# A one-token attention and FFN kernel: wq in two transfers, the Exp table loaded in the preamble, block 0's softmax chain ahead of K1's transposes, and the two halves of H back to back

## The chip, the core and the metric

The kernel runs on one core of a Trainium2 chip. The metric is the time of one execution on the device in microseconds; the median of three runs is 112.3 us.

The engines are named as in the profile: PE is TensorE, DVE is VectorE, ACT is ScalarE, POOL is GpSimd, and SP is SyncE, which here only issues transfers.

## What is computed

Two rows x (batch 2, one token, D = 448) go through a normalisation, attention over a window of a cache, a small FFN, and a gate:

```python
W = min(4096, max(256, Sk // 4))                       # 2048 of 8192 cached positions
q = (xn @ wq).reshape(B, Sq, 16, 256)                  # xn = layernorm(x); wq [448, 4096]
scores = einsum("bhqd,bhkd->bhqk", q, k) * 256 ** -0.5 # 8 K/V heads, each used by 2 query heads
o = einsum("bhqk,bhkd->bhqd", softmax(scores), v)
s = o.reshape(B, Sq, 4096) @ wo                        # wo [4096, 448]
g = silu(relu(xn @ w1) @ w2)                           # w1 [448, 1792], w2 [1792, 448]
out = x + s * g
```

Everything is bf16 in memory. K and V of the window are 33.6 MB of the 44.1 MB that the kernel reads; wq and wo are 3.7 MB each, w1 and w2 1.6 MB each.

## The kernel before

**Blocks.** The 16 pairs of batch and K/V head are worked on in four blocks of four pairs (`NQ = 4`). K and V of a block are one transfer each of 4 MB, 32 KB for each of the 128 partitions: 32 groups of 64 positions by 4 pairs. There are two K buffers (`kbuf`), one V buffer (`vbuf`), one buffer for weights (`wbuf`: first wq, later w1 and w2), and wo goes into `kbuf[0]` at the end.

**What one block does.** `do_T` (L424) transposes K in eight pieces on DVE (`kt`). `do_S` (L432) makes the scores on PE: one matmul that sets a mask (`wcol`, `wrow`), then 32 of 128x512 into the bank `sbk`, four for each transposed piece. The softmax chain follows: `ch_max` (row maximum, DVE), `ch_rmT` (transpose of the maxima, PE), `ch_mrow` (maximum per pair and a copy, DVE), `ch_exp` (a small matmul, a bias copy and the Exp on ACT, then a sum over partitions on PE), `ch_pt` (transpose of the weights `pt` and the reciprocal of the sum, DVE). `do_PV` (L446) multiplies with V (32 matmuls into `obk`), scales by the reciprocal on ACT (`o_sb`), and folds; `do_at` stores the block's result. `do_qbd` (L360) places the query of a block on POOL.

**The order.** Each engine runs a list of its own, written out by hand: an engine works strictly in the order in which the operations are recorded at L499 to L601, and waits on semaphores. On PE the sections S, PV and CH are loops over the same code, in the order PRO, S(0), CH(0), S(1), PV(0), CH(1), S(2), PV(1), CH(2), S(3), PV(2), CH(3), FFN, PV(3), WO, END. On DVE, block 0's chain is interleaved with the transposes of K1 (L508 to L520): T(1,0), maximum, T(1,1), mrow, T(1,2), T(1,3), T(1,4), pt, reciprocal, T(1,5) to T(1,7). For the later blocks the chain stands ahead of the next block's transposes.

**Transfers.** SP issues all large ones on one queue, in this order: wq, K0, K1, V0, K2 (after K0's last transpose), V1 (after PV(0)), K3 (after K1's last transpose), V2, w1, w2 (after PV(1)), V3 (after PV(2)), and wo in four parts. ACT issues the two small loads of x and the store.

**Start.** ACT clears four banks, DVE makes the statistics of x, ACT takes the square root (L312), DVE builds the normalised row in the layout of the projection (`xr`, L347). `do_q` (L357) multiplies it with wq in seven slots of four matmuls (28 into `fbk`), DVE scales and transposes the query.

**FFN.** `do_H(0)` and `do_H(1)` (L380) are seven matmuls each, for two halves of the hidden row, into `fbk` and `cbk`; after each DVE writes the relu into `h_n`. `do_hT` (L391) transposes `h_n` at once and copies it into `h_sb` in four pieces; `do_F` multiplies with w2 (14 matmuls), `do_gate` applies silu. **End.** The folded result is multiplied with wo: 26 wide matmuls into `wbk` (the first 18 need wo's first part, eight more its second), a copy `wsum` (L575), 4 matmuls that add it and 24 narrow ones into `cbk`, of which the last ones need wo's last parts; then DVE multiplies with the gate (L595), adds x and ACT stores.

All matmuls but one are recorded by the helper `mm`, so the profile has them on L354.

Of the kernel before, what the change touches and what calls it, by code (L numbers as in the profile page):

```python
# [6 lines left out]
F32 = mybir.dt.float32  # L7
ACT = mybir.ActivationFunctionType
# [149 lines left out]
def bass_recurrent_scan__sliding_block_cached__dense_activation_relu__decode_kernel(  # L158
# [34 lines left out]
    with es:  # L193
# [26 lines left out]
        xt = named("xt", [128, SLOTS * 128], BF)  # L220
        st6 = named("st6", [128, 6], F32)
        st2 = named("st2", [128, 2], F32)
        sd = named("sd", [128, 2], F32)
        rstd = named("rstd", [128, 1], F32)
        xr = named("xr", [128, SLOTS * 4], BF)
        qn = named("qn", [128, 512], BF)
# [52 lines left out]
        def load_v(k):  # L279
# [3 lines left out]
        p_xc = pr.op(POOL, lambda e: e.memset(x_c[:, :], 0.0))  # L283
        d_xc = pr.dma(ACTE, view(x_c, 0, [[1, NCOL]], n=8, pstep=16),
                      A_x[:, 0, :].rearrange("b (i n) -> i b n", i=4), [p_xc], key="v")
        d_wq = pr.dma(SP, wbuf[:, :], wq_src)
        load_k(0)
        load_k(1)
        load_v(0)
# [10 lines left out]
        for t0 in (h_sb, h_n, ea, ga):  # L300
# [9 lines left out]
        v_ve = pr.op(DVE, lambda e: e.tensor_scalar(  # L310
            out=sd[0:B, 0:1], in0=st2[0:B, 1:2], scalar1=EPS, scalar2=None, op0=ALU.add), [v_ag])
        a_sd = pr.op(ACTE, lambda e: e.activation(sd[0:B, 1:2], sd[0:B, 0:1], ACT.Sqrt), [v_ve])  # L312
        v_rs = pr.op(DVE, lambda e: e.reciprocal(rstd[0:B, :], sd[0:B, 1:2]), [a_sd])
        for e2 in range(2):
            v_xn = pr.op(DVE, lambda e, e2=e2: e.tensor_scalar(
# [39 lines left out]
                                      skip_group_check=True, **kw)  # L355

        def do_q():  # L357
            deps = [d_wq, v_xr]
            for s in range(SLOTS):
                for i in range(4):  # L360
                    lo = s * HC + i * 512
                    o = pr.op(PE, mm(fbk[32 * i:32 * i + 4, :], xr[:, 4 * s:4 * s + 4], wbuf[:, lo:lo + 512],
                                     s == 0, s == SLOTS - 1, tile_position=(0, 32 * i)), deps)
                    deps = []
            st["q_mm"] = o
            v = pr.op(DVE, lambda e: e.tensor_scalar(
                out=view(qn, 0, [[64, 8], [32, 2], [1, 32]]),
                in0=view(fbk, 0, [[64, 8], [1, 2], [2, 32]]),
                scalar1=SCALE, scalar2=None, op0=ALU.mult), [o])
            st["qT"] = pr.op(DVE, lambda e: e.transpose(qt[:, :], qn[:, :]), [v])  # L370
# [7 lines left out]
                deps = []  # L378

        def do_H(u):  # L380
            deps = [d_w1] if u == 0 else [st["h_n"]]
            for s in range(SLOTS):
                lo = s * FC + u * (FC // 2)
                o = pr.op(PE, mm((fbk, cbk)[u][0:4, 0:FC // 2], xr[:, 4 * s:4 * s + 4], wbuf[:, lo:lo + FC // 2],
                                 s == 0, s == SLOTS - 1), deps)
                deps = []
            st["h_n"] = pr.op(DVE, lambda e: e.tensor_scalar(  # L387
                out=view(h_n, 32 * u, [[64, 14], [1, 32]], n=4), in0=view((fbk, cbk)[u], 0, [[1, 14], [14, 32]], n=4),
                scalar1=0.0, scalar2=None, op0=ALU.max), [o, p_z])

        def do_hT():  # L391
            v = pr.op(DVE, lambda e: e.transpose(ht[0:32, :], h_n[0:32, :]), [st["h_n"]])  # L392
            for hf in range(2):
                for u in range(2):
                    st["hT"] = pr.op(DVE, lambda e, hf=hf, u=u: e.tensor_copy(  # L395
                        view(h_sb, 0, [[1, 14], [16, 2]], n=32, p0=64 * hf + 32 * u),
                        view(ht, 32 * u + hf, [[64, 14], [2, 2]], n=32)), [v, p_z])

        def do_F():
            deps = [d_w2, st["hT"]]  # L400
# [104 lines left out]
        do_S(0)  # L505
        load_k(2)
        do_qbd(1)
        do_T(1, 0)  # L508
        ch_max(0)
        do_T(1, 1)  # L510
        pr.section("CH", 0)
        ch_rmT(0)
        ch_mrow(0)
        do_T(1, 2)
        ch_exp(0)
        do_T(1, 3)
# [115 lines left out]
```

## Time and profile before

| | |
|---|---|
| runs | 112.3, 113.17, 112.0 us; median 112.3 |
| the profiled execution | 112.89 us, of which the span from the first to the last instruction is 111.6 |
| mean granted TensorE clock | 0.816 |
| busy | PE 66.5 us (60%), DVE 58.3 (52%), ACT 14.7 (13%), POOL 7.2 (6%) |
| read from memory | 44.11 MB, 395 GB/s over the span; the SP queue's packets fill 93.2% of 16 engines' time |

How to read the rows: a row of the timeline has the start, the length, engine and line, the operation as result<-operands, the shapes and a count; the bracket at its end is the idle time of the engine before it and what ended that. A row of the windows has the stretch, its length, the busy time (and count) of PE, PEld (weight loads), DVE, ACT and POOL, the granted clock, the DMA share and GB/s; a packet is counted where it begins. The slices of the page are 40 equal parts of the span, the busy share and the granted clock in tenths. A row of DMA issues has the queue, the size, and the median time from issue to landing.

### The profile page before, as it was taken

Reading aid. Unit: us, or ns where it says so; the run is one execution under the profiler, and the core shown is the slowest. Engines: PE = TensorE matmul, PEld = TensorE weight load, DVE = VectorE, ACT = ScalarE, POOL = GpSimd, SP = SyncE. Lnnn points to the kernel's source line nnn. Section 1 sums busy time; section 2 is a strip of 40 time slices with the busy share of each in tenths; the row PEclk is TensorE's granted clock in tenths of the full one; section 3 lists DMA queues with packets and bytes.
Section 4 is the critical chain, followed back from the end, with each engine's and each line's share of the span. In section 5 each row is a group of like instructions: output and inputs, shape, how many; then the busy total and the mean of one; then the engine's idle time right before and its main releaser. Section 6 shows DMA issues by size and latency. Waiting matters only on the chain.

```text
span 111.6 us, 1080 instructions
## 1 busy us (share of the span) xinstructions
PE 66.5 (60%) x412; PEld 25.7 (23%) x412; DVE 58.3 (52%) x94; ACT 14.7 (13%) x32; POOL 7.2 (6%) x31
## 2 busy tenths in 40 slices
PE   0000570069952399992499992349994579099461
PEld 0000110024411233431233431113431312034120
DVE  1089331199979992022799722299952220900531
ACT  2940000000001600004100003200002300002600
POOL 6500003000030000030000030000000000000000
PEclk9999999557999557999656999656999755558999
DMA  6899999999999999976899899899889989979940
GB/s 164 350 443 430 446 423 446 446 411 423 470 411 399 470 435 411 446 305 188 388 493 435 376 458 482 376 423 505 388 378 432 530 376 399 517 330 436 384 189 1
DMA packets 2188, 44.11 MB, mean 395 GB/s; under 512 B 266, under 2 KB 396, under 8 KB 652
## 3 DMA queue, kind: packets, MB, share of 16 engines
q1 hardware_dynamic: 2160, 44.11, 93.2%
q10 hardware_dynamic: 28, 0.01, 0.0%
HBM read 44.11 MB, written 0.00 MB: 395 GB/s over the span
## 4 chain that ended last, share of the span: by engine, by line
DMA 46%; PE 35%; DVE 9%; ACT 4%; issue 3%; SPq 1%; DVEq 0%; ACTq 0%
DMA kbuf<-in_A_k_cache_dram 46%; PE sbk L354 17%; PE fbk L354 6%; PE obk L354 5%; PE cbk L354 3%; DVE kt L429 3%; PE nbk L354 2%; SPq L46 1%; PE wbk L354 1%; ACT o_sb L455 1%; ACT L485 1%; DVE h_n L387 1%; DVE ht L392 1%; ACT e_sb L485 1%; PE mbk L354 1%
## 5 line engine op out<-in xcount | busy, mean ns | idle before, releaser
L354 PE MATMUL sbk<-kt,qbd 128*128 128x512 bf16 x128 | 36.2, 447 | 11.0 <-DVE kt L429 10.9
L429 DVE STREAM_TRANSPOSE kt<-kbuf 128x1024 f32<-128x1024 f32 x32 | 36.8, 1206 | 7.0 <-DMA kbuf<-in_A_k_cache_dram 7.0
L354 PEld LDWEIGHTS sbk<-kt,qbd 128*128 128x128 bf16 x128 | 13.5, 110 | 33.7 <-issue 22.0
L354 PE MATMUL fbk<-wbuf,xr 128*4 128x512 bf16 (+1 forms) x35 | 5.9, 614 | 12.4 <-DVE xr L347 12.4
L354 PE MATMUL obk<-vbuf,pt 128*16 128x512 bf16 x128 | 8.2, 379 | 0.0
L455 ACT ACTIVATE o_sb<-obk,rs 128x512 bf16<-128x512 f32 x4 | 2.7, 687 | 40.2 <-PE obk L354 40.2
L375 POOL COPY qbd<-qt 32x64 bf16<-32x64 bf16 x16 | 3.8, 240 | 58.2 <-PE sbk L354 44.8
L467 DVE TENSOR_REDUCE rm<-sbk 128x1 f32<-128x512 f32 x4 | 2.7, 682 | 8.7 <-PE sbk L354 8.7
L354 PE MATMUL fbk<-wbuf,h_sb 128*17 128x448 bf16 x14 | 4.6, 505 | 2.9 <-DVE h_sb L395 2.9
L354 PE MATMUL nbk<-ssum,gsum 128*128 128x1 f32 x8 | 2.1, 337 | 5.8 <-ACT e_sb L485 5.8
L490 DVE STREAM_TRANSPOSE pt<-e_sb 128x512 bf16<-128x512 bf16 x4 | 2.8, 698 | 4.8 <-ACT e_sb L485 4.8
L484 ACT ACTIVATE bias<-mbk 128x1 f32<-128x1 f32 x4 | 0.7, 171 | 33.4 <-PE mbk L354 33.4
L354 PEld LDWEIGHTS fbk<-wbuf,xr 128*4 128x4 bf16 x35 | 1.6, 114 | 15.0 <-DMA wbuf<-in_A_wq_dram 12.4
L494 DVE TENSOR_TENSOR at_exp<-nbk,qmask 128x64 bf16<-128x64 f32 x4 | 0.9, 225 | 7.2 <-PE nbk L354 7.2
L354 PEld LDWEIGHTS obk<-vbuf,pt 128*16 128x16 bf16 x128 | 3.1, 88 | 4.3 <-issue 1.3
L354 PE MATMUL mbk<-one_f,mrow 1*128 1x1 f32 x8 | 1.5, 256 | 3.4 <-DVE mrow L479 3.4
L415 DVE TENSOR_SCALAR ea<-ea 128x112 f32<-128x112 f32 x1 | 0.2, 219 | 5.8 <-ACT ea L409 5.8
L354 PE MATMUL nbk<-fold,o_sb 128*128 128x8 bf16 x16 | 1.0, 173 | 3.7 <-ACT o_sb L455 3.7
L354 PEld LDWEIGHTS nbk<-ssum,gsum 128*128 128x128 f32 x8 | 1.8, 280 | 6.1 <-ACT e_sb L485 6.1
L354 PE MATMUL cbk<-wbuf,xr 128*4 128x448 bf16 x7 | 2.8, 574 | 0.7 <-DVE h_n L387 0.7
L354 PEld LDWEIGHTS fbk<-wbuf,h_sb 128*17 128x17 bf16 x14 | 1.6, 121 | 6.2 <-issue 6.0
L409 ACT ACTIVATE ea<-fbk 17x112 f32<-17x112 f32 x4 | 1.0, 252 | 14.4 <-PE fbk L354 14.3
(74 smaller groups left out, 42.1 us busy)
## 6 DMA issues: line engine op xcount, KB each, us to landing
kbuf<-in_A_k_cache_dram SPq DMA_DIRECT2D x4, 4096.0 KB, 21.2
vbuf<-in_A_v_cache_dram SPq DMA_DIRECT2D x4, 4096.0 KB
wbuf<-in_A_wq_dram SPq DMA_DIRECT2D x1, 3584.0 KB, 11.5
wbuf<-in_B_w_dram SPq DMA_DIRECT2D x2, 1568.0 KB, 20.0
kbuf<-in_A_wo_dram SPq DMA_DIRECT2D x1, 2016.0 KB, 19.0
kbuf<-in_A_wo_dram SPq DMA_DIRECT2D x1, 896.0 KB, 20.6
kbuf<-in_A_wo_dram SPq DMA_DIRECT2D x1, 448.0 KB, 21.2
kbuf<-in_A_wo_dram SPq DMA_DIRECT2D x1, 224.0 KB, 21.3
```

The lines of the kernel that those rows point to most:

```text
L46: o = _Op(eng, lambda e: e.dma_start(dst, src), deps, True, key)
L354: return lambda e: e.matmul(out_ap, lhsT=lhsT, rhs=rhs, start=start, stop=stop, skip_group_check=True, **kw)
L375: st["qbd", k] = pr.op(POOL, lambda e, a=a: e.tensor_copy(view(qbd, 24 + 32 * a, [[128, 8], [2, 4], [1, 2]], n=32, p0=32 * a), view(qt, 0, ...
L387: st["h_n"] = pr.op(DVE, lambda e: e.tensor_scalar(out=view(h_n, 32 * u, [[64, 14], [1, 32]], n=4), in0=view((fbk, cbk)[u], 0, [[1, 14], [ ...
L392: v = pr.op(DVE, lambda e: e.transpose(ht[0:32, :], h_n[0:32, :]), [st["h_n"]])
L409: a_e = pr.op(ACTE, lambda e, i=i: e.activation(ea[32 * i:32 * i + 17, :], fbk[0:17, i * NCOL:(i + 1) * NCOL], ACT.Exp, scale=-1.0), [st[" ...
L429: st["T", k, e] = pr.op(DVE, lambda e: e.transpose(view(dst, lo, [[128, NT // 2], [1, 32]]), view(src, lo, [[128, NT // 2], [1, 32]])), de ...
L455: st["osb", k] = pr.op(ACTE, lambda e: e.activation(o_sb[:, :], obk[:, :], ACT.Copy, scale=rs[:, k:k + 1]), [st["PV", k], st["rs", k]], ke ...
L467: st["rm", k] = pr.op(DVE, lambda e: e.tensor_reduce(out=rm[:, :], in_=sbk[:, :], axis=AX.X, op=ALU.max), [st["S", k, 7]], key="rm")
L485: st["exp", k] = pr.op(ACTE, lambda e: e.activation(e_sb[:, :], sbk[:, :], ACT.Exp, bias=bias[:, 0:1], accum_out=ssum[:, 0:1]), [a], key=" ...
L490: st["pt", k] = pr.op(DVE, lambda e: e.transpose(pt[:, :], e_sb[:, :]), [st["exp", k]], key="pt")
L494: st["at", k] = pr.op(DVE, lambda e: e.tensor_tensor(out=view(at_exp, 16 * k, [[64, 4], [4, 4], [1, 4]]), in0=view(nbk, 0, [[4, 4], [1, 4] ...
```

## The change

wq is loaded by two transfers, its first slot alone and the other six; the projection waits for the first before slot 0 and for the second before slot 1. An Exp on a spare column is recorded right after the square root, so that the Exp table is loaded there and not before block 0's softmax. On DVE, block 0's maximum and mrow come before the first transpose of K1; T(1,0) follows them, T(1,1) follows the Exp, T(1,2) to T(1,7) follow pt and the reciprocal; on PE the order stays the same. H(1) no longer waits for the relu of H(0), and each half's `h_n` is transposed and copied by itself, between the halves and after them. The rest is as before.

```diff
-        sd = named("sd", [128, 2], F32)
+        sd = named("sd", [128, 3], F32)
...
-        d_wq = pr.dma(SP, wbuf[:, :], wq_src)
+        d_wq = [pr.dma(SP, wbuf[:, lo * HC:hi * HC], wq_src[:, lo * HC:hi * HC]) for lo, hi in ((0, 1), (1, SLOTS))]
...
         a_sd = pr.op(ACTE, lambda e: e.activation(sd[0:B, 1:2], sd[0:B, 0:1], ACT.Sqrt), [v_ve])
+        pr.op(ACTE, lambda e: e.activation(sd[0:B, 2:3], sd[0:B, 0:1], ACT.Exp))
...
         def do_q():
-            deps = [d_wq, v_xr]
+            deps = [d_wq[0], v_xr]
             for s in range(SLOTS):
+                if s == 1:
+                    deps = [d_wq[1]]
...
         def do_H(u):
-            deps = [d_w1] if u == 0 else [st["h_n"]]
+            deps = [d_w1] if u == 0 else []
...
-        def do_hT():
-            v = pr.op(DVE, lambda e: e.transpose(ht[0:32, :], h_n[0:32, :]), [st["h_n"]])
+        def do_hT(u):
+            v = pr.op(DVE, lambda e: e.transpose(
+                view(ht, 32 * u, [[64, 14], [1, 32]], n=32), view(h_n, 32 * u, [[64, 14], [1, 32]], n=32)),
+                [st["h_n"]])
             for hf in range(2):
-                for u in range(2):
-                    st["hT"] = pr.op(DVE, lambda e, hf=hf, u=u: e.tensor_copy(
...
+                st["hT"] = pr.op(DVE, lambda e, hf=hf: e.tensor_copy(
...
         do_qbd(1)
-        do_T(1, 0)
         ch_max(0)
-        do_T(1, 1)
         pr.section("CH", 0)
         ch_rmT(0)
         ch_mrow(0)
-        do_T(1, 2)
+        do_T(1, 0)
         ch_exp(0)
-        do_T(1, 3)
-        do_T(1, 4)
+        do_T(1, 1)
         ch_pt(0)
-        for e in range(5, 8):
+        for e in range(2, 8):
             do_T(1, e)
...
         do_H(0)
+        do_hT(0)
         do_H(1)
-        do_hT()
+        do_hT(1)
```

More of the change, by code (lines that the diff above doesn't have):

```diff
@@ L389, in do_H @@
                 scalar1=0.0, scalar2=None, op0=ALU.max), [o, p_z])
-        def do_hT():
-            v = pr.op(DVE, lambda e: e.transpose(ht[0:32, :], h_n[0:32, :]), [st["h_n"]])
+        def do_hT(u):
+            v = pr.op(DVE, lambda e: e.transpose(
+                view(ht, 32 * u, [[64, 14], [1, 32]], n=32), view(h_n, 32 * u, [[64, 14], [1, 32]], n=32)),
+                [st["h_n"]])
             for hf in range(2):
-                for u in range(2):
-                    st["hT"] = pr.op(DVE, lambda e, hf=hf, u=u: e.tensor_copy(
-                        view(h_sb, 0, [[1, 14], [16, 2]], n=32, p0=64 * hf + 32 * u),
-                        view(ht, 32 * u + hf, [[64, 14], [2, 2]], n=32)), [v, p_z])
+                st["hT"] = pr.op(DVE, lambda e, hf=hf: e.tensor_copy(
+                    view(h_sb, 0, [[1, 14], [16, 2]], n=32, p0=64 * hf + 32 * u),
+                    view(ht, 32 * u + hf, [[64, 14], [2, 2]], n=32)), [v, p_z])
         def do_F():
```

## The prediction

> **What bounds the kernel now.** I read the page first (slices, DMA issues), then the half-microsecond windows around the poorest slices, then the timeline.
>
> ```profile
> span 111.6 us, 1080 instructions
> PEclk9999999557999557999656999656999755558999
> GB/s 164 350 443 430 446 423 446 446 411 423 470 411 399 470 435 411 446 305 188 388 493 435 376 458 482 376 423 505 388 378 432 530 376 399 517 330 436 384 189 1
> ...
> kbuf<-in_A_wo_dram SPq DMA_DIRECT2D x1, 896.0 KB, 20.6
> ...
> kbuf<-in_A_wo_dram SPq DMA_DIRECT2D x1, 224.0 KB, 21.3
> ```
>
> A slice is 2.79 us. After the start, GB/s stays around 430 but for the 18th and 19th slice (47.4 to 53.0 us): 305 and 188. The windows there (last columns: DMA share, GB/s):
>
> ```profile
> 49.50:50.00 0.50, 0.50 (x12) 0.10 (x4) 0.00 (x0) 0.00 (x0) 0.00 (x0) 1.00 0.01 0
> ...
> 51.00:51.50 0.50, 0.37 (x5) 0.16 (x5) 0.23 (x2) 0.00 (x0) 0.00 (x0) 1.00 0.00 0
> 51.50:52.00 0.50, 0.00 (x0) 0.00 (x0) 0.40 (x2) 0.00 (x0) 0.00 (x0) 1.00 2.09 524
> ```
>
> For 2.0 us no packet begins. The transposes that wait for K give the pace of the stream, and the queue of SP gives the reason:
>
> ```profile
> 22.03 9.13 DVE L429 STREAM_TRANSPOSE kt<-kbuf 128x1024 f32<-128x1024 f32 x8 [4.99 <-DMA kbuf<-in_A_k_cache_dram]
> ...
> 31.77 1.25 DVE L429 STREAM_TRANSPOSE kt<-kbuf 128x1024 f32<-128x1024 f32 x1 [0.62 <-DMA kbuf<-in_A_k_cache_dram]
> ...
> 72.57 9.13 DVE L429 STREAM_TRANSPOSE kt<-kbuf 128x1024 f32<-128x1024 f32 x8 [1.41 <-DMA kbuf<-in_A_k_cache_dram]
> ```
>
> ```profile
> SPq L46 <- PE obk L354: 50.1, 3, 18.4
> ```
>
> ```profile
> 31.18 0.54 SPq L46 DMA_DIRECT2D kbuf<-in_A_k_cache_dram  x1
> ...
> 50.17 0.54 SPq L46 DMA_DIRECT2D vbuf<-in_A_v_cache_dram  x1
> ...
> 84.68 0.55 SPq L46 DMA_DIRECT2D vbuf<-in_A_v_cache_dram  x1
> ```
>
> K0 and K1 landed 31.77 - 22.03 = 9.74 us apart: 4.19 MB at 431 GB/s. From K1 to K3 the queue brings V0, K2, V1, K3: four transfers, 38.96 us, but it took 40.80. So 1.84 us (2.0 by the windows; I take 1.9) the 16 engines had nothing queued, because SP may issue V1 (50.17) only when block 0's PV has freed the one V buffer. K2, issued at 31.18, was the last in the queue. Everywhere else the stream is continuous: it is the bound, with one hole. Without the hole V1 must be issued by 50.17 - 1.9 = 48.3. What leads to PV of block 0:
>
> ```profile
> 23.42 8.83 PE L354 MATMUL sbk<-kt,qbd 128*128 128x512 bf16 x32 [7.33 <-DVE kt L429]
> ...
> 32.94 0.65 DVE L467 TENSOR_REDUCE rm<-sbk 128x1 f32<-128x512 f32 x1
> ...
> 34.66 0.24 DVE L476 TENSOR_REDUCE mx<-mbk 1x8 f32<-1x128 f32 x1
> ...
> 35.94 1.28 ACT L485 ACT_TABLE_LOAD   x1
> ...
> 38.58 0.60 PE L354 MATMUL sbk<-wcol,wrow 4*128 4x512 bf16 x1
> 39.12 9.18 PE L354 MATMUL sbk<-kt,qbd 128*128 128x512 bf16 x32
> ...
> 48.23 1.90 PE L354 MATMUL obk<-vbuf,pt 128*16 128x512 bf16 x32
> ```
>
> S(0) ends at 32.25, but the row maximum starts only at 32.94, behind K1's first transpose (31.77), and the second maximum (34.66) behind another one; then a table load of 1.28; S(1) starts at 38.58, PV(0) at 48.23, V1 is issued 1.94 later. Block 1's chain shows what it costs undisturbed:
>
> ```profile
> 51.10 0.27 PE L471 MATMUL mbk<-ident_f,rm 128*1 128x128 f32 x1
> ...
> 51.79 0.21 DVE L479 COPY mrow<-mx 1x128 f32<-1x128 f32 x1
> ...
> 54.08 0.60 PE L354 MATMUL sbk<-wcol,wrow 4*128 4x512 bf16 x1
> ```
>
> From the transpose of the maxima (51.10) to the end of mrow 0.90, to the next S 2.98 us.
>
> **The change, part by part.**
>
> *Exp table and order of block 0.* The table load goes to ScalarE behind Sqrt in the preamble, where ScalarE has nothing more to do until block 0's bias, just ahead of that load: cost 0, and 1.28 leave the chain. The maximum now starts about 0.1 after S(0) (32.35, 0.65 long), its transpose at 33.1; mrow ends at 34.0; S(1) begins at 33.1 + 2.98 = 36.1, 2.5 earlier. The price is on VectorE: K1's first transpose waits behind mrow, 34.05 in place of 31.77. Two transposes end at 36.4 (9.13 / 8 = 1.14 each), pt and the reciprocal at 37.25, six more at 44.1, 1.4 later than now. Behind these waits stand only K1's transposes and S(1); K3, which needs K1's buffer, stands behind V1 on SP and loses nothing. K2's issue follows K0's last transpose as before; POOL's qbd for block 1 is released by the end of S(0).
> S(1)'s end has two limits. VectorE:
>
> ```profile
> 73.96 8.84 PE L354 MATMUL sbk<-kt,qbd 128*128 128x512 bf16 x32 [2.64 <-DVE kt L429]
> ```
>
> S(3) ends at 82.80, 1.1 after its last transpose (72.57 + 9.13), so 44.1 + 1.1 = 45.2. TensorE: data matmuls from 36.6, by 8.84 (S(3)) to 9.18 (S(1) now): 45.4 to 45.8. I take 45.5; V1 is issued 1.94 later, 47.4, 0.9 before the hole would open. The hole goes: everything behind V1 in the queue lands 1.9 earlier. V0 (31.77 + 9.74 = 41.5) is there for PV(0). Block 2 does not become late: K2 lands at 31.77 + 2 x 9.74 = 51.25, and its transposes, now at 54.3, would be free for it then.
>
> *The halves of H.*
>
> ```profile
> 88.59 2.77 PE L354 MATMUL fbk<-wbuf,xr 128*4 128x448 bf16 x7
> ...
> 92.06 2.77 PE L354 MATMUL cbk<-wbuf,xr 128*4 128x448 bf16 x7 [0.70 <-DVE h_n L387]
> ...
> 94.88 0.61 DVE L387 TENSOR_SCALAR h_n<-cbk 4x448 bf16<-4x448 f32 x1 [2.87 <-PE cbk L354]
> 95.52 1.10 DVE L392 STREAM_TRANSPOSE ht<-h_n 32x896 bf16<-32x896 bf16 x1
> 96.66 0.93 DVE L395 COPY h_sb<-ht 32x28 bf16<-32x28 bf16 x4
> ```
>
> H(1) no longer waits for h_n(0): 92.06 - 91.36 = 0.7. The first half's h_n, transpose and two copies (about 0.6 + 0.6 + 0.46 = 1.7) lie beside H(1)'s 2.77. After H(1) remain 0.61, half a transpose (0.55 by halving 1.10) and two copies of four: 0.95 less. F starts 1.65 earlier against the end of block 3's chain.
>
> *wq in two.*
>
> ```profile
> 12.39 3.15 PE L354 MATMUL fbk<-wbuf,xr 128*4 128x512 bf16 x28 [12.39 <-DVE xr L347]
> ...
> 17.10 1.07 POOL L375 COPY qbd<-qt 32x64 bf16<-32x64 bf16 x4 [12.86 <-DVE qt L370]
> ```
>
> ```profile
> L46 SPq DMA_DIRECT2D kbuf<-in_A_wo_dram x4: 432/442/591, 85.3 to 86.9; - x4
> ```
>
> The projection is released by xr at 12.39, not by wq, so an early first slot gains 0. Were the second piece late, the 5.2 us between qbd's end (18.17) and S(0)'s first data matmul (23.42) hide it; block 1's qbd, of the same size, is done at 33.4 and needed at 36.6. The second issue delays K0's by about 0.4 us, while wq fills the queue until 12. On the stream: wo's last three transfers (second issue about 85.9, last 86.9) landed at 106.5 and 108.2, so 672 KB of short rows in 1.7 us, 395 GB/s; 512 KB of wq at that rate cost 0.1 more. Lower end -0.5 (the first two slices, 164 and 350, lose 2.3 us to a slow start, which a small first piece may change; no row shows how), upper end +0.5 likewise. I take +0.1. [...]
>
> *The end.*
>
> ```profile
> 104.48 0.69 ACT L455 ACTIVATE o_sb<-obk,rs 128x512 bf16<-128x512 f32 x1
> ...
> 106.33 1.49 PE L354 MATMUL wbk<-kbuf,at 128*2 128x448 bf16 x26 [0.32 <-DVE at L568]
> 107.86 0.62 DVE L575 COPY wsum<-wbk 128x448 f32<-128x448 f32 x1 [1.59 <-PE wbk L354]
> ...
> 109.27 0.27 DVE L595 TENSOR_TENSOR tmp<-cbk,g_sb 128x112 f32<-128x112 f32 x1 [0.78 <-PE cbk L354]
> ```
>
> Now arithmetic is last: the last wo lands at 108.2, and the closing multiply starts at 109.27. After: the second wo part lands at 106.5 - 1.9 = 104.6; eight of 26 wide matmuls after it take about 0.7; from wsum to the multiply 109.27 - 107.86 = 1.41: 106.7, 2.55 earlier. The last part (106.3) plus about 0.3 says the same. For this the o_sb of 104.48 must come by about 101.6 (1.85 to the wide matmuls, 18 of them in 1.1), 2.9 earlier: K3's landing gives 1.9, H 1.65, together 3.55, less 0.34 if S(3) then takes S(1)'s 9.18. So H's edit is covered work once the DMA binds; without it the end would come some 1.0 later.
>
> **Sum:** -2.55 + 0.1 = -2.45. The profiled execution has 112.89 (span 111.6 and 1.3 around it): 110.4. The median of the runs, 112.3, is 0.6 below it, and no row says why; I take a part of that over: 110.2.
>
> **Rivals.**
> A. The hole closes only partly, because the clock rises late in S(1). PEclk falls to 5 in the 14th slice (36.3) and rises in the 16th (41.9 to 44.6), while S(1) has its data from 39.12. If it rises at the same moment though S(1) starts 2.5 earlier, 2.5 us more pass at half speed and cost 1.25: S(1) ends at 45.8 + 1.25 = 47.1, V1 goes at 49.0, 0.7 of the hole stays: 110.9; with the rise half a slice later, 111.6. For it: the moment of the rise is not in the program's hand. Against: 0.9 us of slack, and S(3), which started 1.4 after its first transpose like the others, took only 8.84. [...]
> B. The second piece of wq does not follow without a gap. V1 into an empty queue took 1.3 to 1.8 us from its issue to its first packets (50.17 to the window of 51.50): 111.5 to 112.0. Against: the wo rows.
> C. The hole reopens ahead of V3. K3's landing 1.9 earlier (70.6), V2 (9.74) and 3.2 MB of w1 and w2 (7.4) empty the queue at 87.8; as V1 needed 51.25 - 48.3 = 2.9 before K2's landing, V3 must be issued by 84.8. It is issued at 84.68 now and should come at 82.8 to 83.1. Were S(3) so much slower that V3 went 2 us after 84.8, the hole would be back: 112.2. Against: 1.7 us of slack, and the stages' spread of 0.34.
> D. Slower. From 32.25 to 36.1 TensorE works on three small matmuls, and S(1) could stay at half clock to its end. At half clock its weight loads stand 0.43 apart:
>
> ```profile
> 39.95 0.14 PEld L354 LDWEIGHTS sbk<-kt,qbd 128*128 128x128 bf16 x1 [0.28 <-issue]
> 40.38 0.14 PEld L354 LDWEIGHTS sbk<-kt,qbd 128*128 128x128 bf16 x1 [0.28 <-issue]
> ```
>
> 32 x 0.43 = 13.7: S(1) ends at 50.3, V1 goes at 52.2, 2 us later than now: 112.9 + 2.0 - 0.7 (the arithmetic's lag at the end, gone with H's edit) = 114.2. It decides once S(1) ends after 48.3. Against: PEclk rises during each of the four S.
> E. Better: the small first piece shortens the start of the stream by 0.6: 109.6.
>
> **How the numbers follow.** Forecast 0.68 (110.2, own range 109.7 to 110.7), A 0.15, B 0.05, C 0.03, D 0.03, E 0.06. A measurement of this kernel tells about 1% from no change: 111.2 and 113.4. Faster: forecast, E and two thirds of A, 0.84; same: the rest of A, B and C, 0.13; slower: D, 0.03. The range 109.4 to 111.4 holds forecast, E and nearly all of A.
>
> **What would show it.** No window without packets around 50 us; V1's issue at about 47.4; S(1) from about 36.1; no table load in block 0's chain; K3's first transpose at 70.6 to 70.7; H(1) right behind H(0); F 1.65 us closer to H(0); the closing multiply at about 106.7, released through wo's landing. Wrong it would be if V1 is issued after 48.3, if K0's first transpose moves by more than 0.3 from 22.03, or if transfers take longer than 9.74 each.

## The result, and the profile after

| | before | after |
|---|---|---|
| median of 18 runs each, us | 112.93 (111.73 to 113.90) | 111.25 (109.95 to 113.45) |
| ratio after to before, with 95% interval | | 0.9854 [0.9817, 0.9892] |
| the profiled execution, us (its span) | 112.89 (111.6) | 109.95 (108.4) |
| start of the closing multiply, us | 109.27 | 106.06 |

The change gains 1.7 us in the median: 111.25, where 110.2 was forecast. That lies inside the whole range, 109.4 to 111.4, but outside the forecast's own, 109.7 to 110.7. The profiled execution is the fastest of the 18 after: it gains 2.9. So the mechanism must be read from the profile, and the other 1.3 us (111.25 - 109.95) from what most executions do differently. The ratios leave out runs more than 1.5% above the fastest of their kernel, but these show no lower granted clock (0.851 to 0.884 after, where the others have 0.801 to 0.907) and four of the profiles below are of such runs, so I give medians of all runs beside the ratios.

The page of after's profile, same rows as before. In the slices (2.71 us each), GB/s has no dip such as the 305 and 188 of before:

```profile
span 108.4 us, 1083 instructions
...
PEclk9999999656999769997559999558999556959999
...
GB/s 81 431 427 429 472 472 399 399 448 496 399 387 435 508 411 387 423 508 423 387 387 448 520 387 387 423 532 399 387 389 431 535 411 387 411 437 411 396 281 1
```

The windows of 12 us (after the stretch: busy time of PE, PEld, DVE, ACT, POOL, then granted clock, DMA share, GB/s) that hold the hole, of before and then of after: 347 and 431 GB/s.

```profile
46.00:58.00 12.00, 8.36 (x59) 3.48 (x58) 5.71 (x10) 1.64 (x4) 0.96 (x4) 0.82 0.85 347
```

```profile
46.00:58.00 12.00, 8.11 (x38) 2.99 (x27) 8.68 (x12) 1.64 (x4) 0.00 (x0) 0.72 1.01 431
```

The timeline of after, block 0's chain and the stream:

```profile
21.57 9.13 DVE L433 STREAM_TRANSPOSE kt<-kbuf 128x1024 f32<-128x1024 f32 x8 [4.52 <-DMA kbuf<-in_A_k_cache_dram]
...
22.96 8.84 PE L355 MATMUL sbk<-kt,qbd 128*128 128x512 bf16 x32 [6.86 <-DVE kt L433]
...
31.91 0.69 DVE L471 TENSOR_REDUCE rm<-sbk 128x1 f32<-128x512 f32 x1 [1.21 <-PE sbk L355]
...
33.34 0.21 DVE L483 COPY mrow<-mx 1x128 f32<-1x128 f32 x1
33.48 2.35 DVE L433 STREAM_TRANSPOSE kt<-kbuf 128x1024 f32<-128x1024 f32 x2
...
35.83 8.80 PE L355 MATMUL sbk<-kt,qbd 128*128 128x512 bf16 x32
36.42 6.83 DVE L433 STREAM_TRANSPOSE kt<-kbuf 128x1024 f32<-128x1024 f32 x6
...
44.56 1.90 PE L355 MATMUL obk<-vbuf,pt 128*16 128x512 bf16 x32
...
46.51 0.54 SPq L46 DMA_DIRECT2D vbuf<-in_A_v_cache_dram  x1
...
70.14 9.13 DVE L433 STREAM_TRANSPOSE kt<-kbuf 128x1024 f32<-128x1024 f32 x8 [2.40 <-DMA kbuf<-in_A_k_cache_dram]
```

The row maximum starts at once (31.91), S(1) has its data at 35.83 in place of 39.12, and V1 goes at 46.51 in place of 50.17. From K0's first transpose to K3's lie five transfers of 4 MB: 70.14 - 21.57 = 48.57, 9.71 each, against 72.57 - 22.03 = 50.54 before. This difference is my measure below: what exceeds 48.57 (and the time of bytes that a variant adds in between) is time that the stream lost. Before: 1.97. After: 0 by this definition. The packets bear that out: each engine carries eight packets of 32 KB of a transfer, 1.213 us each at the median, together 9.70.

The end of after:

```profile
86.15 2.77 PE L355 MATMUL fbk<-wbuf,xr 128*4 128x448 bf16 x7
...
88.72 2.73 PE L355 MATMUL cbk<-wbuf,xr 128*4 128x448 bf16 x7
...
88.96 0.61 DVE L390 TENSOR_SCALAR h_n<-fbk 4x448 bf16<-4x448 f32 x1 [2.51 <-PE fbk L355]
89.61 0.63 DVE L395 STREAM_TRANSPOSE ht<-h_n 32x448 bf16<-32x448 bf16 x1
90.27 0.46 DVE L399 COPY h_sb<-ht 32x28 bf16<-32x28 bf16 x2
...
93.40 4.20 PE L355 MATMUL fbk<-wbuf,h_sb 128*17 128x448 bf16 x14 [1.95 <-DVE h_sb L399]
...
99.79 0.69 ACT L459 ACTIVATE o_sb<-obk,rs 128x512 bf16<-128x512 f32 x1
...
101.95 1.11 PE L355 MATMUL wbk<-kbuf,at 128*2 128x448 bf16 x18 [0.62 <-DMA kbuf<-in_A_wo_dram]
...
104.04 0.55 PE L355 MATMUL wbk<-kbuf,at 128*2 128x448 bf16 x8 [0.98 <-DMA kbuf<-in_A_wo_dram]
104.64 0.62 DVE L577 COPY wsum<-wbk 128x448 f32<-128x448 f32 x1 [3.06 <-PE wbk L355]
106.06 0.27 DVE L597 TENSOR_TENSOR tmp<-cbk,g_sb 128x112 f32<-128x112 f32 x1 [0.79 <-PE cbk L355]
```

H(1) follows H(0) directly, half of h_n, ht and h_sb lies beside it, and the wide matmuls (18 and 8) now wait for wo: DMA is last to the end, as forecast. K3's first transpose to the closing multiply takes 35.92, 0.78 less than before. The three parts add up: 0.46 (K0's first transpose is earlier) + 1.97 (the hole) + 0.78 (the end) = 3.21 = 109.27 - 106.06.

### The profile page after: what moved, and what is told of

It reads as the page before. It is cut to its first block, busy times and chain, and to the rows that moved or that the text cites. A ratio compares the mean times of both kernels' runs of the same rounds, so it can differ in the third digit from the quotient of the medians.

```text
span 108.4 us, 1083 instructions
## 1 busy us (share of the span) xinstructions
PE 65.6 (61%) x412; PEld 25.4 (23%) x412; DVE 58.7 (54%) x95; ACT 14.9 (14%) x33; POOL 7.2 (7%) x31
## 4 chain that ended last, share of the span: by engine, by line
DMA 58%; PE 23%; DVE 12%; SPq 2%; issue 1%; ACT 1%; DVEq 0%; ACTq 0%
DMA kbuf<-in_A_k_cache_dram 39%; DMA kbuf<-in_A_wo_dram 19%; PE sbk L355 18%; DVE kt L433 10%; PE obk L355 3%; SPq L46 2%; ACT e_sb L489 1%; PE cbk L355 1%; DVE rm L471 1%; DVE wsum L577 1%; PE wbk L355 1%; PE mbk L355 0%; PE nbk L355 0%; DVE mx L480 0%; DVE tmp L597 0%
## 5 line engine op out<-in xcount | busy, mean ns | idle before, releaser
L433 DVE STREAM_TRANSPOSE kt<-kbuf 128x1024 f32<-128x1024 f32 x32 | 36.6, 1205 | 6.9 <-DMA kbuf<-in_A_k_cache_dram 6.9
L489 ACT ACTIVATE e_sb<-sbk,bias 128x512 bf16<-128x512 f32 x4 | 2.7, 687 | 0.4
L355 PE MATMUL wbk<-kbuf,at 128*2 128x448 bf16 x26 | 1.7, 352 | 1.6 <-DMA kbuf<-in_A_wo_dram 1.6
```

The lines of the kernel that those rows point to most:

```text
L355: return lambda e: e.matmul(out_ap, lhsT=lhsT, rhs=rhs, start=start, stop=stop, skip_group_check=True, **kw)
L433: st["T", k, e] = pr.op(DVE, lambda e: e.transpose(view(dst, lo, [[128, NT // 2], [1, 32]]), view(src, lo, [[128, NT // 2], [1, 32]])), de ...
L489: st["exp", k] = pr.op(ACTE, lambda e: e.activation(e_sb[:, :], sbk[:, :], ACT.Exp, bias=bias[:, 0:1], accum_out=ssum[:, 0:1]), [a], key=" ...
```

## Experiments

Theory after the result: the hole is closed in the profiled execution because its V1 went early enough; in others V1 goes later, since PE's clock rises at another moment in S(0) and S(1), and part of the hole is back. Rivals: the gain comes from the start (wq) or the end (H) and the order does little; the scatter is that of the machine; it isn't the clock, but the time that the queue needs ahead.

All runs in one table. "Lost" is K3's first transpose minus K0's, minus 48.57, minus the filler's time at 432 GB/s where a variant puts other bytes ahead of V1. "Lead" is how long V1's issue (that of its first half, where V comes in halves) stands ahead of the nominal end of K2's transfer (and the filler's): K0's first transpose + 3 x 9.71 + filler - issue. Both are of the profiled execution. "Kernel before" is its median on the same chip.

| kernel | median, us | kernel before | ratio [95%] | K0's first transpose | V1's issue | K3's first transpose | lead | lost |
|---|---|---|---|---|---|---|---|---|
| before | 112.93 | | | 22.03 | 50.17 | 72.57 | 1.00 | 1.97 |
| after | 111.25 | 112.93 | 0.9854 [0.9817, 0.9892] | 21.57 | 46.51 | 70.14 | 4.20 | 0 |
| wq in one | 111.84 | 112.98 | 0.9789 [0.9693, 0.9884] | 21.78 | 48.65 | 70.94 | 2.27 | 0.59 |
| old order | 112.41 | 112.98 | 0.9864 [0.9792, 0.9936] | 22.11 | 49.59 | 71.82 | 1.66 | 1.14 |
| old H | 111.69 | 112.98 | 0.9889 [0.9827, 0.9951] | 21.70 | 48.27 | 71.74 | 2.57 | 1.47 |
| filler 5 | 110.61 | 112.98 | 0.9786 [0.9731, 0.9842] | 21.48 | 46.43 | 71.43 | 5.52 | 0.05 |
| after, again | 111.39 | 113.13 | 0.9893 [0.9849, 0.9937] | 21.89 | 46.98 | 71.45 | 4.05 | 0.99 |
| warm PE, twice | 111.97 | 113.13 | 0.9984 [0.9938, 1.0030] | 21.83 | 46.49 | 71.34 | 4.48 | 0.94 |
| V in halves | 111.46 | 113.13 | 0.9898 [0.9792, 1.0003] | 21.95 | 47.96 | 70.98 | 3.13 | 0.46 |
| halves and warm | 112.14 | 113.13 | 0.9973 [0.9939, 1.0007] | 21.71 | 45.49 | 71.61 | 5.36 | 1.33 |
| warm PE, chain | 111.83 | 113.17 | 0.9897 [0.9800, 0.9993] | 21.83 | 47.11 | 71.76 | 3.86 | 1.36 |
| filler 6 and 6 | 110.47 | 113.17 | 0.9832 [0.9747, 0.9916] | 21.82 | 47.00 | 72.03 | 5.56 | 0.05 |
| filler 8 and 8 | 110.54 | 113.17 | 0.9838 [0.9773, 0.9902] | 21.78 | 46.99 | 72.53 | 6.06 | 0.06 |
| filler 8 and 8, again | 110.67 | 113.16 | 0.9798 [0.9749, 0.9848] | 21.91 | 49.08 | 72.67 | 4.10 | 0.07 |

**wq in one transfer** (the changed kernel without that part):

```diff
-        d_wq = [pr.dma(SP, wbuf[:, lo * HC:hi * HC], wq_src[:, lo * HC:hi * HC]) for lo, hi in ((0, 1), (1, SLOTS))]
+        d_wq = pr.dma(SP, wbuf[:, :], wq_src)
...
```

> The changed kernel with wq again in one transfer. Theory (the stream of transfers binds, and the small first piece only shortens its start): K0's first transpose goes back from 21.57 to about 22.0, every later landing with it, and the time is 0.4 to 0.5 us above the changed kernel's, ratio to the kernel before about 0.989. Rival (the split only moves an early wait that is hidden): K0's transpose stays near 21.6 and the time is the changed kernel's.

```profile
21.78 9.13 DVE L431 STREAM_TRANSPOSE kt<-kbuf 128x1024 f32<-128x1024 f32 x8 [4.73 <-DMA kbuf<-in_A_k_cache_dram]
```

K0's first transpose came at 21.78, not at the 22.0 of the theory. The twelve kernels in the table with two transfers lie at 21.48 to 22.11, the two with one at 22.03 and 21.78: the split has no effect on the start of the stream that these runs can tell. The 0.46 by which the profiled pair differs lies within that spread.

**The old order of block 0** (K1's transposes between the steps of the chain, as before):

```diff
+        do_T(1, 0)
         ch_max(0)
+        do_T(1, 1)
...
-        do_T(1, 0)
+        do_T(1, 2)
...
-        do_T(1, 1)
+        do_T(1, 3)
+        do_T(1, 4)
...
-        for e in range(2, 8):
+        for e in range(5, 8):
```

> The changed kernel with block 0's chain and K1's transposes in the order of before; the Exp table stays in the preamble. Theory: S(1) starts about 37.0 (1.5 later than in the changed kernel's profile), V1 is issued at about 47.7 to 49.0, so a hole of 0 to 1.0 us is left in the stream, and the time is 0.3 to 1.0 above the changed kernel's. Rival (the early table alone closes the hole): no hole and no difference.

```profile
23.50 9.84 PE L355 MATMUL sbk<-kt,qbd 128*128 128x512 bf16 x32 [7.62 <-DVE kt L433]
...
38.53 9.17 PE L355 MATMUL sbk<-kt,qbd 128*128 128x512 bf16 x32
...
49.59 0.54 SPq L46 DMA_DIRECT2D vbuf<-in_A_v_cache_dram  x1
```

```profile
46.00:58.00 12.00, 8.36 (x57) 3.38 (x56) 6.29 (x10) 1.64 (x4) 0.96 (x4) 0.79 0.94 390
```

With the table load gone but the transposes back in front of the chain, S(1) has its data at 38.53, V1 goes at 49.59, and the hole is back (1.14 lost, 390 GB/s). How much of the gain is the table's and how much the order's can't be read from V1 (50.17, 49.59, 46.51), since S(0) took 1.01 longer here than before. From the end of S(0) to the data of S(1) it is 6.87 before, 5.19 here and 4.03 in after. So 1.68 went with the table, of which the load itself is 1.28, and 1.16 with the order. Before, K1's first transpose also held up the maximum (it started 0.69 after S(0)); here S(0) ended so late that it didn't (0.11). So the two parts are of about the same size. By the medians the old order costs about 1 us (112.41 against 111.25 and 111.39), from eight runs.

**The old H** (H(1) waits for the relu of H(0); one transpose of both halves):

```diff
-            deps = [d_w1] if u == 0 else []
+            deps = [d_w1] if u == 0 else [st["h_n"]]
...
-        do_hT(0)
         do_H(1)
-        do_hT(1)
+        do_hT()
```

> The changed kernel with the FFN's halves as before (H(1) waits for the first relu, one transpose, four copies). Theory (the end is set by wo's landing, and H's edit only keeps arithmetic ahead of it): F starts 1.65 later against H(0), the wide matmuls start at about 103 in place of 101.95, but the eight behind wo's second part still start at its landing, and the time rises by 0 to 0.3. Rival (arithmetic binds the end): the closing multiply comes 1.65 later and the time rises by as much.

```profile
87.76 2.77 PE L355 MATMUL fbk<-wbuf,xr 128*4 128x448 bf16 x7
...
91.23 2.77 PE L355 MATMUL cbk<-wbuf,xr 128*4 128x448 bf16 x7 [0.70 <-DVE h_n L390]
...
96.90 3.78 PE L355 MATMUL fbk<-wbuf,h_sb 128*17 128x448 bf16 x12 [2.89 <-DVE h_sb L398]
...
103.24 0.69 ACT L458 ACTIVATE o_sb<-obk,rs 128x512 bf16<-128x512 f32 x1
...
105.09 1.49 PE L355 MATMUL wbk<-kbuf,at 128*2 128x448 bf16 x26 [0.32 <-DVE at L568]
...
108.03 0.28 DVE L595 TENSOR_TENSOR tmp<-cbk,g_sb 128x112 f32<-128x112 f32 x1 [0.78 <-PE cbk L355]
```

F starts 9.14 after H(0) (96.90 - 87.76), against 7.25 in after: the edit moves F by 1.89. At the end it is worth less. Here the 26 wide matmuls run in one piece without a wait for wo, and the multiply starts 36.29 after K3's first transpose, against 35.92: 0.37. The other 1.5 us lie in after's own waits for wo. (V1 went late in this execution, and 1.47 were lost; that shifts both ends of this difference alike.) And 0.37 is the worth in after's own execution: the same stretch takes 36.75 with wq in one and 37.26 in the changed kernel again, both with H's new halves, so there the old H would have been the faster end. Why is shown below.

**Filler 5**: five of w2's fourteen columns of 448 (573 KB, 1.33 us) are loaded ahead of V1, when the queue would otherwise be empty, and the other nine in w2's place. w2's part of the buffer is free since the projection. It tests the hole by itself: bytes that have to be moved anyway cover a late V1, whatever makes it late.

```diff
...
+        d_w2a = pr.dma(SP, wbuf[:, W2:W2 + 5 * D], w2_src[:, 0:5 * D], [st["q_mm"]])
...
-                d_w2 = pr.dma(SP, wbuf[:, W2:W2 + 14 * D], w2_src)
+                d_w2 = pr.dma(SP, wbuf[:, W2 + 5 * D:W2 + 14 * D], w2_src[:, 5 * D:14 * D])
```

> The changed kernel with the first 5 of 14 columns of w2 (0.57 MB, 1.3 us of the stream) loaded between K2 and V1 in place of with the rest after w1. Theory A (in most runs of the changed kernel V1 is issued too late for a part, because S(1)'s clock rises at another moment than in the profiled run, and the hole is open by some tenths to 1 us): the filler covers it, the median falls from a ratio of 0.985 to about 0.975 and comes near the profiled run's 110. Rival R (the stream itself is slower in those runs, or its end later): no hole to fill, the ratio stays at 0.985.

Nothing is lost at V1 (0.05), and the median is 110.61. V3, issued at 83.73, was now itself short of lead, and by the packets behind it the 16 engines came 0.2 to 0.8 late: rival C's mechanism, in a smaller size.

**The changed kernel, again**, unchanged:

> The changed kernel itself, once more, for a trace of another execution and for times beside the next three. Theory A (the place of the clock's step decides how early V1 is issued; a hole of about 2.8 us less the time from V1's issue to K2's landing stays open): in this trace S(1) takes 8.8 to 9.6 us, and the spacing of V1's landing to K2's is 9.71 plus that hole. Rival R (the stream itself is slower in the longer runs): spacing over 9.71 also where nothing waits. Ratio to the kernel before again 0.98 to 0.99.

```profile
21.89 9.13 DVE L433 STREAM_TRANSPOSE kt<-kbuf 128x1024 f32<-128x1024 f32 x8 [4.83 <-DMA kbuf<-in_A_k_cache_dram]
...
36.30 8.80 PE L355 MATMUL sbk<-kt,qbd 128*128 128x512 bf16 x32
...
46.98 0.53 SPq L46 DMA_DIRECT2D vbuf<-in_A_v_cache_dram  x1
```

```profile
46.00:58.00 12.00, 8.00 (x44) 3.03 (x33) 8.21 (x12) 1.64 (x4) 0.24 (x1) 0.72 1.00 415
```

This is the most telling run: the same kernel, S(1) as long as in after, V1 at 46.98, only 0.47 later than in after and well before the 48.3 of the prediction, and still 0.99 lost, where the theory put down ahead of it (2.8 less the lead) leaves nothing to lose. The records of the single packets show how many of the 16 DMA engines have one in hand: 13 from 49.8 to 51.1. Three engines stand idle until 51.08 to 51.18, 4.1 to 4.2 us after V1's issue, though K2's packets are done on them, and two packets of V1 took 2.36 and 2.46 us in place of 1.21. In after all 16 are busy the whole time. K3's transfer then ends between 69.42 and 71.00 on the 16 engines, where in after it ends between 69.14 and 69.57. The end of this execution shows a second loss:

```profile
105.88 0.92 PE L355 MATMUL wbk<-kbuf,at 128*2 128x448 bf16 x8 [0.99 <-DMA kbuf<-in_A_wo_dram]
...
108.71 0.27 DVE L597 TENSOR_TENSOR tmp<-cbk,g_sb 128x112 f32<-128x112 f32 x1 [1.23 <-PE cbk L355]
```

```profile
105.80:108.80 3.00, 2.05 (x40) 0.95 (x40) 0.72 (x2) 0.00 (x0) 0.00 (x0) 0.50 0.05 21
```

```profile
104.00:106.20 2.20, 1.23 (x40) 0.62 (x40) 0.77 (x2) 0.00 (x0) 0.00 (x0) 1.00 0.41 153
```

From the eight last wide matmuls to the multiply it takes 2.83, in after 2.02: the granted clock is 0.50 here and 1.00 there. All of the difference between the two multiplies, 108.71 - 106.06 = 2.65, is now placed: 0.32 by K0's first transpose, 0.99 at V1, 0.53 up to the wide matmuls (one engine late once more, at V3) and 0.81 at the end. The windows of the other kernels show when this happens. In nine profiles the wide matmuls wait for wo: after has a clock of 1.00 behind that wait, warm PE in the chain 0.81, warm PE twice 0.57, and the six others (wq in one, old order, filler 5, this one, and the two with halves) 0.50. In the five in which they don't wait (before, old H, the three with filler ahead of V3) it is 1.00.

**Warm PE, twice**: 20 matmuls of 128x512 into an unused bank ahead of S(0) and 10 in each block's chain (3, 3 and 4), work that the result doesn't need, meant to have the granted clock up when S(0) and S(1) begin.

```diff
...
+        def spin(n, deps=()):
+            for _ in range(n):
+                pr.op(PE, mm(jbk[:, :], ident[:, :], junk[:, :], True, True), deps)
...
+        spin(20, [p_j])
...
```

> The changed kernel with extra matmuls on constant data into an unused bank, whose results nobody reads: 20 after the projection and 10 in each softmax chain, to hold the TensorE clock up between the stages. Theory A: the clock stays at full speed through S(0) and S(1), S(1) ends at the transposes' limit of about 44.6 whatever the place of the clock's step, V1 goes at about 46.6, there is no hole, and the ratio falls to about 0.975 with a narrow spread. Rival R: the clock stays up but the time stays at 0.985. If the clock falls all the same, the extra matmuls cost up to 1 us a chain and the ratio rises towards 0.99.

S(1) took 8.50 (granted clock 1.00 from 34 to 46 us, 0.86 in after) and V1 went at 46.49, as meant, and its 12 spans lie within 110.1 to 111.7. But their median, 110.6, is longer than the changed kernel's 110.0 on the same chip: 0.94 is lost in the profile, and not at V1, where no engine stands idle. The page of its profile has a queue that after's doesn't have:

```profile
q1 hardware_dynamic: 2304, 44.11, 94.0%
q8 instruction: 2, 0.03, 0.1%
```

One of its two packets of 16 KB, at 35.26, occupied one of the 16 engines for 1.04 us in the middle of the stream. V0's transfer then ended at 41.65 on that engine and by 40.67 on the others, K3's at 70.77 and by 69.77: the engine stayed 1.0 behind. That the added code causes the fetch fits (the variant with fewer matmuls, below, has no such packet in the stream) but wasn't tried by itself.

**V in halves**: V is loaded by two transfers, and the first half of V1 is released by the first 16 matmuls of PV(0).

```diff
...
-            d_v[k] = pr.dma(SP, vbuf[:, :], kv_src(k, A_v_cache), [st.get(("PV", k - 1))], key="v")
+            src = kv_src(k, A_v_cache)
+            hw = ROW // 2
+            d_v[k] = pr.dma(SP, vbuf[:, 0:hw], src[:, :, 0:hw] if len(src.shape) == 3 else src[:, 0:hw], [st.get(("PVh", k - 1))], key="v")
+            d_v2[k] = pr.dma(SP, vbuf[:, hw:ROW], src[:, :, hw:ROW] if len(src.shape) == 3 else src[:, hw:ROW], [st.get(("PV", k - 1))], key="v2")
...
```

> The changed kernel with each V load in two halves, of which the first waits only for the first 16 matmuls of the PV before it. Theory A: V1's first half is issued 0.95 us earlier, which closes holes up to that size: ratio about 0.978 to 0.980, V1's issue before 47.7 in nearly every phase of the clock. Rival R, or a cost of the additional transfers: ratio 0.985 or above.

S(1) took 9.51 in this execution, so that even the first half went only at 47.96, past the 47.7 of the theory; 0.46 lost. The median, 111.46, isn't better than after's, so the rival's outcome stands.

**Halves and warm**, both together:

> The extra matmuls of b2_warm and the half loads of c1_half_v together. Theory A: no hole in any run; as b2_warm, ratio about 0.975, since one of the two is enough. Rival R: 0.985.

The first half of V1 went at 45.49, but here too a packet of instructions (at 34.81) held up one engine, for 1.03 us, and 1.33 are lost; the theory's 0.975 was missed again. The lead was ample (5.36) and no engine stood idle at V1: this loss isn't V1's.

**Warm PE, chain**: only the 10 matmuls in each block's chain.

> The changed kernel with the 10 extra matmuls on constant data in the softmax chain alone, a loop's code that is fetched once, and none after the projection. Theory (b2_warm lost its gain to one fetch of 16 KB of instructions that held one of the 16 engines for 1 us): no such packet in the middle of the trace, S(1) takes 8.5 to 8.9 us, V1 goes 0.3 to 1.5 us earlier in the late phases of the clock, and the median is 110.6 to 111.0. Rival (the extra matmuls themselves cost the time): 112, as b2_warm.

```profile
21.83 9.13 DVE L441 STREAM_TRANSPOSE kt<-kbuf 128x1024 f32<-128x1024 f32 x8 [4.77 <-DMA kbuf<-in_A_k_cache_dram]
...
36.72 8.52 PE L358 MATMUL sbk<-kt,qbd 128*128 128x512 bf16 x32
...
47.11 0.54 SPq L46 DMA_DIRECT2D vbuf<-in_A_v_cache_dram  x1
```

```profile
34.00:46.00 12.00, 11.36 (x60) 3.92 (x61) 10.69 (x13) 0.95 (x3) 0.62 (x3) 1.00 0.99 426
46.00:58.00 12.00, 9.26 (x57) 3.44 (x51) 7.55 (x12) 1.64 (x4) 0.34 (x2) 1.00 0.97 404
```

The granted clock is 1.00 through S(1) and beyond, S(1) is as short as in any profile (8.50 to 9.61), no instructions are fetched in the stream, V1 goes at 47.11, within 0.3 of the 47.4 that was forecast, and 1.36 are lost (404 GB/s). By the packets only eight engines are busy from 50.2 to 51.0, and the last of the others starts again at 51.81, 4.7 us after the issue. So an issue at 47.11 was too late here with the clock at 1.00 all through S(1). The clock still has its share in the 47.1: S(0) took 9.45, since the clock rose only at 28.02; with after's 8.84 V1 would have gone at about 46.5. The median, 111.83, is nearer to the rival's 112 than to the theory's 110.6 to 111.0; the spans' median is 109.95, as the changed kernel's: the 10 matmuls gain nothing.

**Filler 6 and 6, filler 8 and 8**: w2's first columns ahead of V1, and wo's first columns (into `kbuf[0]`, free after K2's last transpose) ahead of V3 (the diff is that of 8 and 8).

```diff
...
+        d_w2a = pr.dma(SP, wbuf[:, W2:W2 + 8 * D], w2_src[:, 0:8 * D], [st["q_mm"]])
...
+                d_wo = pr.dma(SP, wo_sb[:, 0:8 * D], wo_src[:, 0:8 * D], [st["T", 2, 7]])
...
```

> The changed kernel with two parts of the weights used to keep the queue filled: 6 of 14 columns of w2 (0.69 MB, 1.6 us of the stream) go between K2 and V1, and 6 of 32 columns of wo (as much) between w2's rest and V3. Theory (a V load issued less than about 3.4 us before the first of the 16 engines runs dry loses up to 1.2 us on some of them, and in most executions V1 and sometimes V3 come that late): from K0's first transpose to K3's pass 5 x 9.71 + 1.6 = 50.2 us with nothing lost, V3's lead stays above 3.4, and the median falls to 110.0 to 110.4, 1 us below the changed kernel's. Rival (the longer executions come from elsewhere, as from instruction fetches): median as the changed kernel's, 111.3.

> The same with 8 and 8 columns (2.1 us each). Theory: V1's lead is safe in every phase of the clock, V3's as before, but V3 lands 2.1 later and PV(3)'s chain comes near wo's landing: 110.0 to 110.6. Rival: 111.3, or above 110.6 if the arithmetic becomes last.

The end with 8 and 8:

```profile
103.94 1.49 PE L355 MATMUL wbk<-kbuf,at 128*2 128x448 bf16 x26 [0.32 <-DVE at L574]
...
106.88 0.28 DVE L601 TENSOR_TENSOR tmp<-cbk,g_sb 128x112 f32<-128x112 f32 x1 [0.78 <-PE cbk L355]
```

Medians 110.47 and 110.54, nothing lost at V1. The price is at the end: V1 and all behind it land later by the filler's 1.6 and 2.1 us, so arithmetic is last again, and the multiply starts at 106.74 and 106.88, against 106.06 in after's profile. But the wide matmuls don't wait, the clock behind them is 1.00, and that is earlier than in the kernels whose end fell to half clock (107.64 with filler 5, 108.71 in the changed kernel again).

**Filler 8 and 8, again**, in new runs:

> The version with eight columns of w2 ahead of V1 and eight columns of wo ahead of V3 once more, in more rounds. My theory (a V transfer must be issued about 3.4 us before the first of the 16 engines runs dry; the fillers give that in any phase of the clock, so the loss of 0 to 1.5 us is gone and with it most of the scatter): all spans within about 0.8 us of each other, around 109.2 to 109.6, median 110.5, ratio to the kernel before 0.975 to 0.985; from K0's first transpose to K3's 50.7 (48.57 and the filler's 2.1). The rival (the scatter of the changed kernel comes from elsewhere, and the six close runs were luck): spans spread over 2 us or more, median 111.2 or above, ratio around 0.985 to 0.99.

```profile
21.91 9.13 DVE L435 STREAM_TRANSPOSE kt<-kbuf 128x1024 f32<-128x1024 f32 x8 [4.88 <-DMA kbuf<-in_A_k_cache_dram]
23.30 9.91 PE L355 MATMUL sbk<-kt,qbd 128*128 128x512 bf16 x32 [7.45 <-DVE kt L435]
...
37.59 9.61 PE L355 MATMUL sbk<-kt,qbd 128*128 128x512 bf16 x32
...
49.08 0.54 SPq L46 DMA_DIRECT2D vbuf<-in_A_v_cache_dram  x1
```

```profile
46.00:58.00 12.00, 8.18 (x57) 3.13 (x56) 6.80 (x11) 1.64 (x4) 0.96 (x4) 0.79 1.00 429
```

By chance the profiled execution had the longest S(0) and S(1) of all: 9.91 and 9.61, V1 at 49.08, 2.6 later than in after. Nothing was lost (0.07, 429 GB/s), where the old order, with V1 at 49.59 and no filler, lost 1.14. Median 110.67 and spans from 108.8 to 110.0: closer than after's, but by 1.2, not the 0.8 that I expected. Over all runs, the 24 spans of the filler kernels have the median 109.3 (108.6 to 110.5), the 30 of the changed kernel 109.95 (108.4 to 112.5). So the fillers beat the changed kernel, by some 0.65 in the median, while after's best execution stays ahead of them. Kernel by kernel the intervals of their ratios (0.9786 to 0.9838) overlap that of after (0.9854), so it is the four together that show it: 22 of the 24 spans lie below 109.95.

## Why the prediction was right, and where not

**Right.** The stream of transfers binds, with one hole, ahead of V1; it was 1.97 by the two traces, 1.9 by the prediction. Order and table: S(1) has its data at 35.83 (forecast 36.6), T(1,0) starts at 33.48 (34.05), K1's transposes end at 43.25 (44.1), V1 goes at 46.51 (47.4), in an execution whose S(0) and S(1) are among the shortest (8.84 and 8.80). H's halves: F 1.89 closer to H(0), forecast 1.65. wq: no cost that shows (+0.1 forecast): K0's first transpose came at 21.48 to 22.11 with two transfers, 21.78 and 22.03 with one. End: bound by wo's landing, 35.92 from K3's first transpose to the multiply (forecast 70.65 to 106.7, 36.05).

**The step that failed** is "Without the hole V1 must be issued by 50.17 - 1.9 = 48.3", and with it "47.4, 0.9 before the hole would open". It took the loss to shrink one for one with an earlier issue: a lead of 1.00 + 1.97 = 2.97 would then lose nothing. For leads up to 2.3 this holds (1.66 lost 1.14, sum 2.80; 2.27 lost 0.59, sum 2.86). For leads from 2.6 to 4.05 it doesn't: 2.57 lost 1.47, 3.13 lost 0.46 (the issue of a first half), 3.86 lost 1.36, 4.05 lost 0.99. Leads of 4.10 and 4.20 lost nothing, nor did any above but for the two with a fetch of instructions (4.48 and 5.36). By this the deadline was about 22.0 + 29.1 - 4.1 = 47.0, and the forecast's 47.4 is on the wrong side of it: a slack of -0.4 in place of 0.9. Missing it cost 0.99 and 1.36 at once, not some tenths.

What the packets show behind it is that V1 started later on a busy queue than on an empty one. The 2.97 comes from before, where the queue was empty: there all 16 engines had begun V1 within 2.18 us of its issue. With the queue still busy, the engines that ran dry stood idle until 4.1 to 4.2 us after the issue (the changed kernel again) and until 4.7 us after it (warm PE in the chain). The 4.1 itself is no sharper than some tenths, because the engines end K2 up to 1.0 us apart (49.50 to 50.47 in the changed kernel again, 49.59 to 50.16 in after). Counted from the first engine that ends the transfer ahead of V1, the changed kernel again and warm PE in the chain have 2.5 us and lost, and 2.7 (filler 8 and 8, again), 3.1 (after) and 3.1 (warm PE, twice) lost nothing there; the 3.4 of the fillers' theory was more than was needed.

**How that gives the median.** From the profiled execution of before, the sum was 110.4. In the profiled execution of after, K0's first transpose came 0.46 earlier where 0.1 later was forecast, the hole gave 0.07 and the end 0.13 more, and the time around the span grew by 0.26: 110.44 - 0.76 + 0.26 = 109.94, as measured. The spans of after have the median 109.9, 1.5 above the profiled one. Two losses that this one escaped are of that size: V1 issued too late (0.5 to 1.5 in six profiles), and the end at half clock (0.81 in the changed kernel again). That the unprofiled executions had them is inferred; how often each occurs isn't shown. The prediction took 0.7 for the wide matmuls and 1.41 from wsum to the multiply from a profile in which PE worked without a wait; it had nothing for a clock at half behind a wait. The prediction also took 0.2 off for the median of before lying below its profiled execution; with 18 runs it doesn't (112.93 and 112.89), so those 0.2 were no effect.

**Rival A** (0.15) named the outcome, 110.9 to 111.6, and half the cause. The median is A's outcome and not the forecast's; the whole range holds it only because it was drawn wide enough to hold A. S(0) took from 8.83 to 9.91 and S(1) from 8.50 to 9.61 in the profiles: together that moves V1 by some 2 us between executions. By the clock's records the granted clock rose at 26.26, 43.33 and 60.40 before: 17.07 apart. After, it rose at 26.38, 40.03 and 57.10: 13.65 and 17.07 apart, four and five times 3.413, the shortest stretch of one clock in its records (0.50 from 36.62 to 40.03). So the rise in S(1) did not stay at its moment, as A had it, but came 3.30 earlier, as S(1) itself did. Over all 14 profiles the rise in S(0) lies anywhere from 25.55 to 29.08, while S(0) starts at 22.88 to 23.50; in the two profiles of filler 8 and 8, one kernel, S(0) starts at 23.17 and 23.30 and takes 9.10 and 9.91. What sets the moment of the rise isn't shown. But the run with the clock held up through S(1) lost 1.36, so at V1 the clock decides how late the issue is, not that 47.1 is too late.

**The other rivals.** B (a gap behind the split wq): not seen. C: V3 goes at 82.24 in after, and nothing was lost there; with the filler at V1 alone V3 became late and lost up to 0.8. D (S(1) at half clock to its end): in none of the profiles. E (a shorter start): K0's first transpose moved by 0.46 in the profiled pair, more than the 0.3 that the prediction allowed, but the other kernels show a spread of that size with or without the split; no effect is shown.

**H's worth at the end** was set at about 1.0 once DMA binds; old H cost 0.37 against after's execution, and nothing against those that end at half clock. Without a wait for wo the multiply follows o_sb by 4.79 (108.03 - 103.24 with old H); after's o_sb at 99.79 would have given 104.58, and 1.48 of the edit's 1.89 are covered by wo, where the prediction had 0.65 of 1.65.

**What stays open.** That the wait for wo is what lowers the clock at the end is argued from the fourteen profiles, not tried by itself. Nor is it settled why a transfer that is issued while others are still moving starts up to 4.7 us later on some engines, and why its first packets there take up to 2.46 us. No run has the new order without the early table load, so the order by itself is known only as a difference. The split by lead rests on one profile for each kernel; the fillers, which raise the lead and nothing else at V1, and whose 24 runs scatter less, are the test of the hole, not of that reason.

## What to carry to other kernels

Here a queue of transfers bound, and the hole ahead of V1 wasn't closed when its issue just met the end of the transfer before: it took about 4 us of lead, and less lost up to 1.5 us (1.47 with 2.57 of lead). Where a queue binds, measure the lead that a load needs. When the issue hangs on arithmetic whose time varies from run to run (here by 2 us with the clock), move bytes that have to be loaded anyway, into space that is already free, ahead of that issue; look then at what they delay, because arithmetic at the end became last here (the multiply at 106.74 and 106.88, after's at 106.06). An end that waits for its last transfer may cost more than the wait: behind it PE's granted clock was below 1.00 in eight of nine profiles, at half for 0.8 us in the one that was added up. And count many runs: one profile showed the gain of 2.9 us, the median 1.7.

## What the runs showed of the hardware that was not expected

- V1 behind other transfers needed more lead than its start on an empty queue suggested: with the queue empty, all 16 engines had begun V1 2.18 us after its issue (before); with it busy, an engine stood idle until 4.7 us after it (warm PE in the chain).
- A DMA engine that fell behind in the stream stayed behind. Each of the 16 engines carries eight packets of 32 KB of a K or V transfer (1.213 us each at the median, in before and after). In warm PE, twice, a packet of instructions occupied one engine for 1.04 us: it ended V0 at 41.65 (the others by 40.67) and K3 at 70.77 (by 69.77), and 0.94 was lost. In before the engines ended K0 from 20.56 to 21.57 and K2 from 49.61 to 50.62, 1.01 apart both times.
- Instructions came over the stream's engines: with the 20 and 10 matmuls of the warm variants came packets of instructions in the midst of the stream (at 35.26 for 1.04 us, 16 KB, and at 34.81 for 1.03 us, on one engine each), and these kernels, whose V1 went early (46.49 and 45.49), weren't faster than the changed kernel on the same chip: medians 111.97 and 112.14 against 111.39, ratios 0.9984 [0.9938, 1.0030] and 0.9973 [0.9939, 1.0007] against 0.9893 [0.9849, 0.9937].
- The 10 matmuls in each block's chain held the granted clock at 1.00 from 34 to 58 us, where it was 0.86 and 0.72 in the same windows of after.
